# Letting a static scheduler choose ScalarE or VectorE for PSUM read-outs in a gated attention and token-mixing kernel

## The chip, the cores and the metric

The kernel runs on one core of a Trainium2 chip. The metric is the device time of one execution in microseconds; lower is better. Three runs of the kernel before gave 779.43, 781.1 and 781.89 us. A separate execution was recorded by the hardware profiler; all rows of a profile below come from such an execution.

## The reference

Two layers, one after the other, on 8 batches of 3200 tokens and 256 channels. Inputs and output are float32.

```python
scores = (1.0 / S) * np.matmul(z, z.transpose(0, 2, 1))   # z: 8 x 3200 x 64
attn = np.maximum(scores, 0.0) ** 2
x = u * np.matmul(attn, v)                                 # u, v: 8 x 3200 x 256
wq, wk = x @ w_q, x @ w_k                                  # 256 x 64 each
W_tok = (1.0 / np.sqrt(64)) * np.einsum('bsd,btd->bst', wq, wk)
mixed = np.einsum('bst,btd->bsd', W_tok, x)
out = np.maximum(mixed, 0.0) @ w_out                       # 256 x 256
```

The token mixing is linear before its relu, so the kernel never forms the 3200 x 3200 matrix `W_tok`: it sums `wk` transposed times `x` over all tokens into a 64 x 256 matrix per batch (the "heads"), and multiplies the queries by that. The score matrix of the first layer is symmetric, so some of its squared blocks are made once and used a second time, turned by a transposing DMA.

## The kernel before

**Tiling.** The tokens of a batch are cut into 25 tiles of 128 and into seven row groups: six of 512 tokens and one of 128. For each group and tile the scores are one 128 x 512 block. Both products of the first layer contract over 64 of the 128 rows of the array, so matmuls are issued in pairs, one on the upper and one on the lower half of the rows, which run side by side. `scores` (L260) makes a pair of blocks into a PSUM slot of two banks; there are two such slots (`pps`, two buffers), shared with the projections, heads, mixing and output products. `first_stage` (L280) reads the slot into `g` (relu and a scale), on VectorE or ScalarE; `second_stage` (L297) squares `g` to `at` in float16, on ScalarE or GpSimd; `second_product` (L346) multiplies `at` (or a turned block `tt`) by `v` into four accumulator banks: two halves of a row group, each with one bank for each half of the array's rows.

**When a half is complete**, `gate` (L362) copies the first bank to SBUF (`both`, L368), adds the second (L369) on VectorE, and multiplies by `u` on GpSimd (`x_sb`, L388). Only then may the next group write those banks. The group's `x` is turned by a DMA on SyncE's queue (`turn_x`, L396); `projections` (L413) makes queries and keys, `projections_out` (L425) casts them to float16 in `qk` (L430); the keys are turned by another DMA and doubled by GpSimd; `heads` (L449) adds their product with `x` to the sum of the batch. When a batch's sum is known, `mix` (L478) and `mix_out` (L490, the relu, L503) and `proj` and `proj_out` (L505, L521) follow while the next batch's attention runs.

**What sets the order.** The order of every engine's instructions is made at build time by a planner written in the kernel (L575 to L1060). It keeps a clock for TensorE, VectorE, ScalarE and GpSimd (`clock`), adds a fixed weight for each piece of work (`give`), and always places the next accumulation step (`acc_step`), pair of scores (`use_pair`) or extra work (`use_keys`, `use_mix`, `use_projs`) on TensorE as its clocks allow. `shut()` is the time at which the open half will be complete; `calm_for` and `choose` keep engines free around it. On the chip the engines follow that order and wait on semaphores; the planner's clocks play no part there. SyncE's queue carries the loads of `u`, all transposing DMAs and the stores; GpSimd's queue those of `v` and `z`.

**Constants of the planner** that the change touches: `KEEP` (L56) is the number of tiles of a row group held back for its last chunk; `XWAIT` (L856) the time between the expected landing of turned `x` and its projections; `MIXES` (L589) the spacing of the three blocks of mixing behind a batch's heads.

Of the kernel before, what the change touches and what calls it, by code (L numbers as in the profile page):

```python
# [16 lines left out]
def kernel(  # L17
# [35 lines left out]
    NX = 7  # L53
    NXT = 4
    NEARBY = 8
    KEEP = 4  # L56

    consts = ctx.enter_context(tc.tile_pool(name="consts", bufs=1))
    pz = ctx.enter_context(tc.tile_pool(name="pz", bufs=1))
# [237 lines left out]
    def second_stage(p, g, ways):  # L297
        at = pat.tile([P, 2 * W], FP16, tag="at", name="at")
        at0 = 0
        parts = pieces(p)  # L300
        if len(ways) > len(parts):
            parts = [(slice(h, h + 1), parts[0][1]) for h in range(2)]
        for (hs, w), on_act in zip(parts, ways * 2):
            n = hs.stop - hs.start
            out = at[:, at0 : at0 + n * w].rearrange("p (n w) -> p n w", w=w)
            if on_act:
                nc.scalar.square(out=out, in_=g[:, hs, 0:w])  # L307
            else:
                nc.gpsimd.tensor_mul(out=out, in0=g[:, hs, 0:w], in1=g[:, hs, 0:w])  # L309
            at0 += n * w  # L310
        at0, blocks = 0, []
        for tile_ in tiles[2 * p : 2 * p + 2]:
            b, gi, ti = tile_
            made[tile_] = (at, at0)
            gj = group_of(ti)
            if is_turned(b, gi, gj):
                blocks.append((b, gi, gj, ti - starts[gj] // P, 1, at0, at0 + widths[gi]))
            at0 += widths[gi]
        if len(blocks) == 2 and blocks[0][:3] == blocks[1][:3] and blocks[1][3] == blocks[0][3] + 1:
            blocks = [blocks[0][:4] + (2, blocks[0][5], blocks[1][6])]  # L320

        def turn(b, gi, gj, n0, nn, c0, c1):
            if (b, gi, gj) not in turned:
                if gj == LASTG:
                    tag, nr, bufs = "ttl", 1, 8
                else:
                    homes[b, gi, gj] = home = homes_free.pop(0)
                    tag, nr, bufs = f"tt{home}", 4, 1
                turned[b, gi, gj] = ptt.tile([P, nr, 4, P], FP16, tag=tag, name=tag, bufs=bufs)
            out = turned[b, gi, gj][:].rearrange("p n j t -> p (n j) t")  # L330
            nc.sync.dma_start_transpose(out=out[:, 4 * n0 : 4 * (n0 + nn), :], in_=at[:, c0:c1])

        return [(x, lambda x=x: turn(*x)) for x in blocks]
# [25 lines left out]

        return [lambda j=j: [one(j, r) for r in range(2)] for j in js]  # L360

    def gate(b, gi, half):  # L362
        if (b, gi) not in xs:
            assert len(xs) < NX, (b, gi, list(xs))
            xs[b, gi] = px.tile([P, 2, NC, 2, dh], FP16, tag="x_sb", name="x_sb")
        n = min(2, widths[gi] // P - 2 * half)
        both = psum.tile([P, 2 * D], FP32, tag="both", name="both")
        nc.scalar.copy(out=both[:, 0 : n * D], in_=accs[half, 0][:, 0 : n * D])  # L368
        nc.vector.tensor_add(  # L369
            out=both[:, 0 : n * D], in0=accs[half, 1][:, 0 : n * D], in1=both[:, 0 : n * D]  # L370
        )
        if b == last and gi >= LASTG - 2:
            if gi == LASTG - 2 and half == 0:
                spare = pv.tile([P, NT, D], FP16, tag="v_sb", name="xd")
                for i in range(3):
                    xds[LASTG - 2 + i] = spare[:, 4 * i : min(4 * i + 4, 9), :]
            nc.vector.tensor_mul(
                out=xds[gi][:, 2 * half : 2 * half + n, :].rearrange("p n d -> p (n d)"),
                in0=both[:, 0 : n * D],
                in1=us[b, gi][:, 2 * half : 2 * half + n, :].rearrange("p n d -> p (n d)"),  # L380
            )
        u_rows = us[b, gi][:, 2 * half : 2 * half + n, :].rearrange("p n (c d) -> p (n c) d", d=dh)
        if 2 * half + n == widths[gi] // P:
            us.pop((b, gi))

        def make_x():
            for r in [half] if widths[gi] == W else range(2):
                nc.gpsimd.tensor_mul(  # L388
                    out=xs[b, gi][:, 0:n, :, r, :].rearrange("p n c d -> p (n c) d"),
                    in0=both[:, 0 : n * D].rearrange("p (m d) -> p m d", d=dh),  # L390
                    in1=u_rows,
                )

        make_x()
# [27 lines left out]
                    stop=(stop and c == NC - 1),  # L422
                )

    def projections_out(b, gi, ps):  # L425
        xTs.pop((b, gi))
        n = min(2, widths[gi] // P)
        qks[b, gi] = pq.tile([P, 2, HW], FP16, tag="qk", name="qk")
        nr = len(halves(gi))
        nc.scalar.copy(out=qks[b, gi][:, 0:nr, 0 : n * P], in_=ps[:, 0:nr, 0 : n * P])  # L430

    def turn_keys(b, gi):
        nn = widths[gi] // P
# [53 lines left out]
                    stop=(db == ND - 1),  # L487
                )

    def mix_out(b, gi, ps):  # L490
        n = min(2, widths[gi] // P)
        nr = len(halves(gi))
        if b < last:
            rts[b, gi] = prt.tile([P, 2, ND, HW], FP16, tag="rt", name="rt")
        else:
            rt = pat.tile([P, 2 * W], FP16, tag="at", name="rt")
            rts[b, gi] = rt[:].rearrange("p (r d s) -> p r d s", r=2, d=ND)
        out = rts[b, gi][:, :, :, :].rearrange("p r d s -> p r (d s)")[:, 0:nr, 0 : ND * n * P]
        if isinstance(ps, list):
            for r in range(nr):  # L500
                nc.scalar.activation(out=out[:, r, :], in_=ps[r][:, 0 : ND * n * P], func=RELU)
        else:
            nc.scalar.activation(out=out, in_=ps[:, 0:nr, 0 : ND * n * P], func=RELU)  # L503

    def proj(b, gi, banks):  # L505
        rt = rts.pop((b, gi))
# [79 lines left out]
    keys_at, out_of, turned_at, z_at, v_at = {}, {}, {}, {}, {}  # L586
    produced, stored = [0], []
    mixed_at = []
    MIXES = 18.0  # L589
    MIXES_END = 14.0  # L590
    PAIRED = [0, 1, 2, 3, 4, 5]
    last = B - 1
# [80 lines left out]
    def squares():  # L673
        while pending and pending[0][0] <= clock[PE] + 0.3:
            ready, p, g = pending.pop(0)
            a, c = max(clock[ACT], ready), max(clock[POOL], ready)
            on_act = a + SPARE < c and (a + 1.06 <= shut() + LATE or a + 2.5 < c)
            ways = [on_act]
            if clock[PE] < UNTIL and max(a + 0.57, c + 0.97) + SPLIT < min(a + 1.06, c + 1.9):
                ways = [a < c, a >= c]  # L680
                done = max(give(ACT, ready, 0.57), give(POOL, ready, 0.97))
            else:
                done = give(ACT, ready, 1.06) if on_act else give(POOL, ready, 1.9)
            for (b, gi, gj, _, nn, _, _), turn in second_stage(p, g, ways):
                n = nn * widths[gi] // P
                due = done + {1: 4.0, 2: 9.0}.get(gj - gi, FARDUE)
# [23 lines left out]
    def use_keys(b, gi):  # L710
# [8 lines left out]
            heads(*prior, ps, halves(gi))  # L719
            clock[PE] += 0.44 if prior[1] < LASTG else 0.11  # L720
        ready = clock[PE] + FROM_PE
        projections_out(b, gi, ps)
        done = give(ACT, ready, 0.56)
        n = widths[gi] / P
        final = (b, gi) == (last, LASTG - 2)
        if not final:
# [37 lines left out]
    def use_mix(b, gi):  # L764
# [1 line left out]
        ps = ps_tile("mx")  # L766
        mix(b, gi, [ps[:, 0, :], ps[:, 1, :]])
        clock[PE] += 0.22
        mix_out(b, gi, ps)
        done = give(ACT, clock[PE] + FROM_PE, 1.03 if gi < LASTG else 0.3)  # L770
        close_slot(done)
        mixed_at.append((done, b, gi))
        if gi in PAIRED:
# [77 lines left out]
            move(max(t + 2, clock[POOL] + SLACK), t + 7, 0.55, 1.6, lambda: load_u(b + 1, 0))  # L851

    SPARE = 0.3
    BIAS = 0.2
    XDUE = 5.0
    XWAIT = 7.0  # L856
    LATE = 0.3

    def half_done(b, gi, half):
        ready = clock[PE] + FROM_PE  # L860
        t = give(ACT, ready, 0.57)
        t = give(DVE, t, 0.68)
        free_at[half] = t
        if b == last and gi >= LASTG - 2:
            give(DVE, t, 0.75)
        t = give(POOL, t, 1.2)
        gate(b, gi, half)
        if half == halves(gi)[-1]:
            n = 8 if widths[gi] == W else 2
            move(  # L870
# [275 lines left out]
```

## Time and profile before

| what | value |
|---|---|
| runs, median (lowest to highest) | 781.1 us (779.43 to 781.89) |
| span of the profiled execution | 780.0 us |
| its instructions | 28,286 |
| mean granted clock of TensorE | 0.998 |

The page gives the busy time and share of each engine, the chain of work that ended last (followed back from the last instruction to whatever released each step), and groups of instructions by source line with their mean duration and the idle time in front of them. PE is TensorE's matmul, PEld its weight load, DVE VectorE, ACT ScalarE, POOL GpSimd and SP SyncE. Further views used below: busy time of each engine in given stretches of the span (with the granted clock, DMA share and GB/s at the end of the row), waits by line and releaser, the chain in order of time, and the timeline.

### The profile page before, as it was taken

What the parts mean: (1) busy time and instruction counts of PE and PEld (TensorE: products, weight loads), DVE (VectorE), ACT (ScalarE), POOL (GpSimd) and SP (SyncE); (2) the same over time, 40 slices, a digit from 0 to 9 for tenths busy, and PEclk for the clock granted to TensorE, in tenths of its full rate; (3) what the DMA queues carried; (4) which work ended last, traced back from release to release, by engine and by line L of the source; (5) the groups of instructions that cost most, each with busy time, mean ns of one, the idle gap of its engine ahead of it and who ended that gap; (6) DMA issues with size and microseconds to landing.
All of it is one profiled execution on the core that took longest, in us unless ns stands there. A gap on an engine that the chain in (4) does not pass through costs nothing.

```text
span 780.0 us, 28286 instructions
## 1 busy us (share of the span) xinstructions
PE 765.9 (98%) x12410; PEld 674.0 (86%) x12410; DVE 490.5 (63%) x506; ACT 558.1 (72%) x672; POOL 619.5 (79%) x518
## 2 busy tenths in 40 slices
PE   8999999999999999999999999999999999999996
PEld 6889989988888888988889888898888988999894
DVE  6576768767565766655657556575566765656534
ACT  6786785676877776876678777787778578777644
POOL 7798887668986978887779769887888868887850
PEclk9999999999999999999999999999999999999999
DMA  7899999999999999999899999999989999989725
GB/s 181 157 152 175 162 160 170 171 187 180 222 183 190 200 218 204 151 170 217 198 171 193 168 221 168 199 161 171 241 159 208 162 196 211 157 169 168 183 81 198
DMA packets 307116, 141.11 MB, mean 181 GB/s; under 512 B 285744, under 2 KB 288432, under 8 KB 306992
## 3 DMA queue, kind: packets, MB, share of 16 engines
q1 hardware_dynamic: 300224, 123.13, 85.8%
q0 software_dynamic: 6624, 15.98, 14.6%
q8 instruction: 97, 1.59, 0.9%
q14 instruction: 27, 0.22, 0.1%
q10 hardware_dynamic: 144, 0.20, 0.1%
HBM read 59.64 MB, written 26.21 MB: 110 GB/s over the span
## 4 chain that ended last, share of the span: by engine, by line
PE 94%; DVE 2%; DMA 1%; ACT 1%; issue 1%; POOL 0%; DVEq 0%; SPq 0%
PE acc L352 68%; PE sc L265 13%; PE fo L513 6%; PE qk L417 3%; PE qk L454 2%; PE mx L482 1%; DVE g L291 1%; DMA v_sb<-in_v_dram 1%; ACT g L287 1%; DVE both L369 0%; DVE fo L535 0%; DMA z<-in_z_dram 0%; ACT at L307 0%; PE xtx L555 0%; PE hd L454 0%
## 5 line engine op out<-in xcount | busy, mean ns | idle before, releaser
L352 PE MATMUL acc<-v_sb,at 64*128 64x256 f16 x7344 | 506.0, 269 | 2.3 <-issue 1.5
L309 POOL TENSOR_TENSOR at<-g 128x1024 f16<-128x1024 f32 (+2 forms) x240 | 432.5, 1813 | 88.0 <-DVE g L291 46.8
L352 PEld LDWEIGHTS <-at 64*128 64x128 f16 x7344 | 403.9, 94 | 54.5 <-issue 9.7
L291 DVE TENSOR_SCALAR g<-sc 128x1024 f32<-128x1024 f32 (+2 forms) x302 | 349.9, 1175 | 121.8 <-PE sc L265 109.8
L307 ACT ACTIVATE at<-g 128x1024 f16<-128x1024 f32 (+2 forms) x242 | 241.6, 1015 | 25.0 <-DVE g L291 22.5
L287 ACT ACTIVATE g<-sc 128x1024 f32<-128x1024 f32 (+2 forms) x177 | 174.8, 990 | 56.2 <-PE sc L265 50.9
L265 PE MATMUL sc<-zT 64*128 64x512 f16 x924 | 185.3, 375 | 2.4 <-DVE g L291 1.2
L388 POOL TENSOR_TENSOR x_sb<-both,u_sb 128x512 f16<-128x512 f32 (+1 forms) x112 | 134.3, 1205 | 48.9 <-DVE both L369 48.4
L352 PE MATMUL acc<-v_sb,tt 64*128 64x256 f16 x2272 | 168.0, 269 | 0.0
L352 PEld LDWEIGHTS <-tt 64*128 64x128 f16 x2272 | 127.0, 94 | 10.3 <-issue 0.6
L369 DVE TENSOR_TENSOR both<-acc,both 128x512 f32<-128x512 f32 (+1 forms) x104 | 69.5, 670 | 70.9 <-ACT both L368 62.0
L368 ACT COPY both<-acc 128x512 f32<-128x512 f32 (+1 forms) x104 | 58.9, 566 | 66.5 <-PE acc L352 63.1
L265 PEld LDWEIGHTS <-zT 64*128 64x128 f16 x924 | 62.2, 94 | 9.8 <-issue 5.2
L535 DVE TENSOR_SCALAR fo<-fo 128x1024 f32<-128x1024 f32 (+2 forms) x31 | 32.7, 1067 | 41.4 <-PE fo L513 41.3
L503 ACT ACTIVATE rt<-mx 128x1024 f16<-128x1024 f32 (+1 forms) x49 | 45.5, 931 | 12.2 <-PE mx L482 12.0
L430 ACT CAST qk<-qk 128x512 f16<-128x512 f32 (+1 forms) x54 | 29.4, 544 | 29.2 <-PE qk L454 25.4
L513 PE MATMUL fo<-wo,rt 128*128 128x256 f16 x400 | 49.4, 273 | 0.1
L469 DVE TENSOR_TENSOR ha<-qk,ha 128x512 f32<-128x512 f32 x37 | 25.6, 691 | 36.1 <-ACT qk L430 35.8
L513 PEld LDWEIGHTS <-rt 128*128 128x128 f16 x400 | 36.4, 98 | 10.8 <-issue 6.5
L540 ACT ACTIVATE fo<-fo 128x1024 f32<-128x1024 f32 (+2 forms) x27 | 24.6, 914 | 19.8 <-PE fo L513 19.8
L417 PE MATMUL qk<-xT_sb,wqk 64*128 64x256 f16 (+1 forms) x404 | 32.2, 265 | 0.0
L454 PE MATMUL qk<-x_sb,kx 64*128 64x256 f16 x360 | 29.1, 269 | 0.0
(44 smaller groups left out, 237.0 us busy)
## 6 DMA issues: line engine op xcount, KB each, us to landing
u_sb<-in_u_dram SPq DMA_DIRECT2D x48, 512.0 KB, 5.0
out_dram<-fo SPq DMA_DIRECT2D x46, 512.0 KB, 4.4
v_sb<-in_v_dram POOLq DMA_DIRECT2D x35, 320.0 KB, 6.2
zn<-in_z_dram POOLq DMA_DIRECT2D x7, 400.0 KB, 6.3
tt<-at SPq DMA_TRANSPOSE x143, 4.5
u_sb<-in_u_dram SPq DMA_DIRECT2D x8, 128.0 KB, 3.6
out_dram<-fo SPq DMA_DIRECT2D x8, 128.0 KB, 3.5
out_dram<-fo SPq DMA_DIRECT2D x4, 256.0 KB, 4.2
```

Source lines behind the costliest of these rows:

```text
L265: nc.tensor.matmul(out=sc[:, h, 0:gw], lhsT=z_cols(b, h, ti * P, P), rhs=z_cols(b, h, gs, gw), start=True, stop=True,)
L287: nc.scalar.activation(out=g[:, hs, 0:w], in_=sc[:, hs, 0:w], func=RELU, scale=GSCALE)
L291: nc.vector.tensor_scalar(out=g[:, hs, 0:w], in0=sc[:, hs, 0:w], scalar1=0.0, scalar2=GSCALE, op0=AOP.max, op1=AOP.mult,)
L307: nc.scalar.square(out=out, in_=g[:, hs, 0:w])
L309: nc.gpsimd.tensor_mul(out=out, in0=g[:, hs, 0:w], in1=g[:, hs, 0:w])
L352: nc.tensor.matmul(out=accs[half, r][:, ds((j % 2) * D, D)], lhsT=weights(b, gi, ti, j)[top(r), :], rhs=vs[b][top(r), ti, :], start=(first ...
L368: nc.scalar.copy(out=both[:, 0 : n * D], in_=accs[half, 0][:, 0 : n * D])
L369: nc.vector.tensor_add(out=both[:, 0 : n * D], in0=accs[half, 1][:, 0 : n * D], in1=both[:, 0 : n * D])
L388: nc.gpsimd.tensor_mul(out=xs[b, gi][:, 0:n, :, r, :].rearrange("p n c d -> p (n c) d"), in0=both[:, 0 : n * D].rearrange("p (m d) -> p m ...
L417: nc.tensor.matmul(out=ps[:, r, 0 : n * P], lhsT=wqk[top(r), c, :, :].rearrange("p t h -> p (t h)"), rhs=xTs[b, gi][top(r), 0:n, c, :], st ...
L503: nc.scalar.activation(out=out, in_=ps[:, 0:nr, 0 : ND * n * P], func=RELU)
L513: nc.tensor.matmul(out=banks[r][:, ds(j * D, D)], lhsT=flat[:, ds((dc * n + j) * P, P)], rhs=wo[:, dc, :], start=(dc == 0 and j == 0), sto ...
```

## The change

Four pieces of work may now go to either of two engines, by the planner's clocks: the copy of the first accumulator bank, the cast of queries and keys and mixing's relu (ScalarE or VectorE), and the square (ScalarE, GpSimd or, under a margin `MORE`, VectorE). The weights in the planner follow (0.58 and 0.69 for a read-out of 512 columns, 1.28 for the product with `u`, others), and `KEEP`, `XWAIT` and `MIXES` have new values.

```diff
-    KEEP = 4
+    KEEP = 6
...
-            if on_act:
+            if on_act == 1:
                 nc.scalar.square(out=out, in_=g[:, hs, 0:w])
             else:
-                nc.gpsimd.tensor_mul(out=out, in0=g[:, hs, 0:w], in1=g[:, hs, 0:w])
+                mul = nc.vector.tensor_mul if on_act else nc.gpsimd.tensor_mul
+                mul(out=out, in0=g[:, hs, 0:w], in1=g[:, hs, 0:w])
...
-    def gate(b, gi, half):
+    def gate(b, gi, half, by_act):
...
-        nc.scalar.copy(out=both[:, 0 : n * D], in_=accs[half, 0][:, 0 : n * D])
+        copy = nc.scalar.copy if by_act else nc.vector.tensor_copy
+        copy(out=both[:, 0 : n * D], in_=accs[half, 0][:, 0 : n * D])
...
-    def projections_out(b, gi, ps):
+    def projections_out(b, gi, ps, by_act=True):
...
-        nc.scalar.copy(out=qks[b, gi][:, 0:nr, 0 : n * P], in_=ps[:, 0:nr, 0 : n * P])
+        copy = nc.scalar.copy if by_act else nc.vector.tensor_copy
+        copy(out=qks[b, gi][:, 0:nr, 0 : n * P], in_=ps[:, 0:nr, 0 : n * P])
...
-            nc.scalar.activation(out=out, in_=ps[:, 0:nr, 0 : ND * n * P], func=RELU)
+            part = ps[:, 0:nr, 0 : ND * n * P]
+            if by_act:
+                nc.scalar.activation(out=out, in_=part, func=RELU)
+            else:
+                nc.vector.tensor_scalar(out=out, in0=part, scalar1=0.0, scalar2=None, op0=AOP.max)
...
-    MIXES = 18.0
+    MIXES = 14.0
...
-            on_act = a + SPARE < c and (a + 1.06 <= shut() + LATE or a + 2.5 < c)
-            ways = [on_act]
+            d = max(clock[DVE], ready)
+            by_act = a + SPARE < c and (a + 1.06 <= shut() + LATE or a + 2.5 < c)
+            by_dve = d + 1.5 + MORE < (a + 1.06 if by_act else c + 1.9) and d + 1.5 <= shut() + LATE + 0.6
+            ways = [2 if by_dve else by_act]
...
-        projections_out(b, gi, ps)
-        done = give(ACT, ready, 0.56)
+        a, d = (max(clock[x], ready) for x in (ACT, DVE))
+        by_act = a + 0.58 <= d + 0.69 or d + 0.69 > shut() + LATE + 0.6
+        projections_out(b, gi, ps, by_act)
+        done = give(ACT, ready, 0.58) if by_act else give(DVE, ready, 0.69)
...
-        mix_out(b, gi, ps)
-        done = give(ACT, clock[PE] + FROM_PE, 1.03 if gi < LASTG else 0.3)
+        ready = clock[PE] + FROM_PE
+        a, d = (max(clock[x], ready) for x in (ACT, DVE))
+        by_act = a + 1.03 <= d + 1.22 or d + 1.22 > shut() + LATE + 0.6
+        mix_out(b, gi, ps, by_act)
+        if by_act:
+            done = give(ACT, ready, 1.03 if gi < LASTG else 0.38)
+        else:
+            done = give(DVE, ready, 1.22 if gi < LASTG else 0.42)
...
+    MORE = 3.0
...
-    XWAIT = 7.0
+    XWAIT = 2.0
...
-        t = give(ACT, ready, 0.57)
-        t = give(DVE, t, 0.68)
+        a, d = (max(clock[x], ready) for x in (ACT, DVE))
+        by_act = max(a + 0.58 + HOP, d) <= d + 0.69
+        t = give(ACT, ready, 0.58) if by_act else give(DVE, ready, 0.69)
+        t = give(DVE, t, 0.69)
         free_at[half] = t
...
-        t = give(POOL, t, 1.2)
-        gate(b, gi, half)
+        t = give(POOL, t, 1.28)
+        gate(b, gi, half, by_act)
```

More of the change, by code (lines that the diff above doesn't have):

```diff
@@ L682, in squares @@
             else:
[L683 removed]
+                done = give(DVE, ready, 1.5) if by_dve else give(ACT, ready, 1.06) if by_act else give(POOL, ready, 1.9)
             for (b, gi, gj, _, nn, _, _), turn in second_stage(p, g, ways):
```

2 lines of the change are left out of this document (1 added, 1 removed).

## The prediction

> **What bounds the kernel now.** I read the page first (busy shares and the chain that ended last), then the busy time in stretches of 20 us, TensorE's own waits, and the chain and the timeline around each hole.
>
> ```profile
> span 780.0 us, 28286 instructions
> PE 765.9 (98%) x12410; PEld 674.0 (86%) x12410; DVE 490.5 (63%) x506; ACT 558.1 (72%) x672; POOL 619.5 (79%) x518
> PE 94%; DVE 2%; DMA 1%; ACT 1%; issue 1%; POOL 0%; DVEq 0%; SPq 0%
> ```
>
> TensorE is busy for 98% of the span and makes 94% of the chain; no other engine is above 79%. A busy TensorE may still be slow, so its pace is needed: the chain has long unbroken pieces.
>
> ```profile
> 74.15 6.22 PE acc L352 x114
> 115.13 1.49 issue
> ```
>
> 114 matmuls of the second product, two at a time on the two halves of the rows, take 6.22 us: 0.109 us a pair. I call this a pair-time below. All other work is fixed in number (both programs have 12,407 matmuls of the same kinds), so only holes in this stream can go or come. Where they are, the stretches tell (engine columns: busy us of 20, instructions):
>
> ```profile
> 0.00:20.00 20.00, 16.17 (x200) 12.53 (x202) 13.49 (x18) 12.76 (x21) 15.49 (x23) 1.00 0.77 183
> 20.00:40.00 20.00, 19.24 (x316) 16.86 (x314) 11.72 (x13) 13.89 (x20) 13.66 (x11) 1.00 0.90 160
> 40.00:60.00 20.00, 19.69 (x319) 17.95 (x318) 15.37 (x15) 17.64 (x20) 19.28 (x15) 1.00 1.03 147
> 60.00:80.00 20.00, 20.00 (x350) 19.62 (x347) 12.53 (x13) 12.33 (x15) 15.54 (x13) 1.00 1.21 167
> ...
> 100.00:120.00 20.00, 18.51 (x313) 17.22 (x311) 13.13 (x14) 15.34 (x17) 16.20 (x15) 1.00 1.30 167
> ...
> 140.00:160.00 20.00, 19.88 (x330) 18.57 (x327) 13.29 (x15) 13.69 (x17) 12.35 (x12) 1.00 1.18 186
> ...
> 400.00:420.00 20.00, 19.47 (x300) 16.81 (x297) 12.53 (x12) 15.56 (x18) 15.88 (x16) 1.00 1.08 190
> ...
> 500.00:520.00 20.00, 19.93 (x337) 18.91 (x334) 14.07 (x14) 15.64 (x20) 17.16 (x14) 1.00 1.13 200
> ...
> 760.00:780.00 20.00, 13.05 (x122) 8.70 (x118) 9.74 (x14) 8.55 (x18) 1.65 (x2) 0.94 0.52 198
> ```
>
> TensorE idles 3.83 us in the first stretch and 6.95 in the last; the middle has 0.76 + 0.31 + 1.49 + 0.12 + 0.53 + 0.07 = 3.28 us, and every stretch left out shows 20.00. The granted clock (1.00) leaves nothing to explain. The idle time understates a hole: a matmul is drawn 0.269 us long (row below), the next is due 0.109 after its start, so each hole costs 0.16 us beyond what is seen. With about sixteen holes in the middle that is 3.28 + 16 x 0.16 = 5.8 us: the most that any reordering can win there.
>
> ```profile
> L352 PE MATMUL acc<-v_sb,at 64*128 64x256 f16 x7344 | 506.0, 269 | 2.3 <-issue 1.5 <-DMA v_sb<-in_v_dram 0.2 <-DVE both L369 0.2
> PE sc L265 <- DVE g L291: 1.2, 5, 0.4
> PE sc L265 <- ACT g L287: 0.9, 3, 0.4
> ```
>
> Eight waits of the scores show as idle. Two kinds of hole matter. One is the score buffer: there are two PSUM slots, and a pair of scores waits until the first stage has read the slot two places back:
>
> ```profile
> 408.07 0.61 PE L265 MATMUL sc<-zT 64*128 64x512 f16 x4
> 408.50 1.23 DVE L291 TENSOR_SCALAR g<-sc 128x1024 f32<-128x1024 f32 x1 [0.48 <-PE sc L265]
> 409.78 0.69 PE L265 MATMUL sc<-zT 64*128 64x512 f16 x4 [0.23 <-DVE g L291]
> ```
>
> The first pair of scores here (512 columns, so two pair-times) is issued by 408.29 and its slot is free at 409.78: about 1.47 us by VectorE, and some 0.2 less by ScalarE (1,025 against 1,220 ns below). The other is the accumulator: the first half must be copied and the second added to it before the next row group may write there.
>
> **The change, part by part.** The prices of what moves (mean ns behind the busy us):
>
> ```profile
> L368 ACT COPY both<-acc 128x512 f32<-128x512 f32 x96 | 55.9, 582 | 64.0 <-PE acc L352 60.8 <-PE sc L265 2.8
> L369 DVE TENSOR_TENSOR both<-acc,both 128x512 f32<-128x512 f32 x96 | 66.2, 690 | 68.5 <-ACT both L368 59.6 <-PE sc L265 6.5 <-PE fo L513 1.8
> L467 DVE COPY ha<-qk 128x512 f32<-128x512 f32 x8 | 5.5, 689 | 5.7 <-ACT qk L430 5.5
> L430 ACT CAST qk<-qk 128x512 f16<-128x512 f32 x47 | 27.5, 585 | 25.4 <-PE qk L454 21.7 <-PE qk L417 3.3
> L503 ACT ACTIVATE rt<-mx 128x1024 f16<-128x1024 f32 x42 | 42.8, 1022 | 11.6 <-PE mx L482 11.4
> L291 DVE TENSOR_SCALAR g<-sc 128x1024 f32<-128x1024 f32 x281 | 339.1, 1220 | 118.0 <-PE sc L265 108.5 <-POOL at L309 2.3 <-POOL x_sb L388 2.2
> L287 ACT ACTIVATE g<-sc 128x1024 f32<-128x1024 f32 x164 | 168.1, 1025 | 49.3 <-PE sc L265 48.4 <-POOL at L309 0.7
> L307 ACT ACTIVATE at<-g 128x1024 f16<-128x1024 f32 x222 | 231.3, 1056 | 24.5 <-DVE g L291 21.9
> L309 POOL TENSOR_TENSOR at<-g 128x1024 f16<-128x1024 f32 x220 | 414.5, 1894 | 86.1 <-DVE g L291 45.3 <-ACT g L287 32.0 <-issue 4.0
> ```
>
> *Who does what.* Counted in the built order of both programs: 41 of 104 accumulator copies, 9 of 54 casts of queries and keys and 3 of 62 relu pieces go to VectorE; first stages go from 302 + 177 (VectorE + ScalarE) to 294 + 184; eight squares go from GpSimd to ScalarE. No square goes to VectorE: the margin MORE = 3.0 is never met, so that part of the edit is empty and costs nothing. ScalarE loses 41 x 0.582 + 9 x 0.585 + 3 x 1.022 = 32.2 us and gains 7 x 1.025 + 8 x 1.056 + one scaling of about 1.0 = 16.6: some 542 us busy. VectorE gains 53 pieces, 41 x 0.689 + 9 x 0.689 + 3 x 1.22 = 38.1, and loses 8 x 1.22 + 1.2 = 11: about 518. GpSimd loses 8 x 1.894 = 15, to 604. All stay below 78% of the span, hidden under TensorE; none of this is on the path except where a reader is late for a slot. The copy and cast on VectorE are priced by the nearest row, the 689 ns copy of the same shape from PSUM; bounds 582 (ScalarE's copy) and 690 (the two-input add). The planner's changed prices (0.58, 0.69) only follow these rows and cost nothing.
>
> *The accumulator.* Copy on ScalarE and add on VectorE take 0.58 + 0.69, both on VectorE 0.69 + 0.69; with hand-overs, and the 0.16 us by which the last matmul outlives its pair-time, about 1.57 and 1.68 us. So VectorE's way is 0.1 longer, and is taken only where ScalarE would be later. KEEP = 6 instead of 4 holds two more tiles back for the closing chunk, 2 x 2 pair-times = 0.44 us more between the end of half 0 and its next use. Counted in the built order behind the first 20 us, half 0 is rewritten within 16 pair-times (1.75 us) seven times before and once after: five times before at only 12 (1.31 us, short by 0.26), and once after, with VectorE's way (short by 0.37).
>
> *The skill on this.* "ScalarE is closer to PSUM, VectorE is closer to SBUF - use accordingly", says the Trainium skill (Advanced Engine Details and Errata, The Read-Write Bubble), which speaks against 53 PSUM reads on VectorE. The rows agree on the sign, 689 against 582 and 1,220 against 1,022: by the rule the sum would be 53 x about 0.11 = 5.9 us worse, if these reads set the end; by the count of covers they don't.
>
> *The score slots.* From 60 us of TensorE work on, five score pairs follow too closely on their slot's readers before (short by 0.05, 0.05, 0.38, 0.18 and 0.16 us), none after. Three of them make most of the 400 to 420 hole. Below 60 us the balance turns: after, four pairs of scores stand close together near 42 us of TensorE work (about 51 us of the span); one slot is rewritten 6 pair-times (0.66 us) behind a VectorE reader that needs 1.47, a wait of 0.81; the next, 4 pair-times behind ScalarE, is paid by the same wait.
>
> *XWAIT 7 to 2, MIXES 18 to 14.* The projections are placed 5 us earlier behind the landing of transposed x: from the close of the accumulator to their first matmul, the middle distance falls from 222 to 166 pair-times (24.2 to 18.1 us). Cover now:
>
> ```profile
> DMA to landing us min/median/max: 2.3/5.5/12.3
> 106.25 2.18 SPq L400 DMA_TRANSPOSE xT_sb<-x_sb  x1
> 125.13 0.27 PE L417 MATMUL qk<-xT_sb,wqk 64*128 64x128 f16 x2
> ```
>
> The slowest transpose is this one: it lands at 106.25 + 12.3 = 118.6 and is used 6.5 us later. Five us less leave 1.5, so both edits cost 0. Without that cover TensorE itself stands, since it works in order (rival C). The moves on SyncE's queue are the same in number and kind. MIXES pulls the second and third mixing blocks 4 and 8 us forward; a buffer of queries and keys still has over 25 us of TensorE work between its last use and its next writer.
>
> *The sum against the profiled execution.* The 400 to 420 stretch: 0.53 idle + four holes x 0.16 = 1.2, all gone (bounds 0.8 and 1.3). Accumulator shortages elsewhere in the middle: two of 0.26 = 0.5 gone; slot shortages of 0.05 and 0.16 = 0.2 gone. Before 60 us: two shortages of 0.26 and one slot wait of 0.16 gone, 0.37 and 0.81 come: +0.5 (bounds -0.7, if the new crowding is absorbed, and +1.5, if squares behind it come late too). The 1.49 us at 115: no semaphore ended it, the kernel's edits don't touch its cause, and the page says only that TensorE waited for nothing that it shows. It is one event in 780 us; I count it as half gone, (1.49 + 0.16)/2 = -0.8, bounds -1.65 and +1.65 (twice). Together -1.2 - 0.5 - 0.2 + 0.5 - 0.8 = -2.2. The first and last stretches stay: the order is unchanged for the first 230 matmuls (200 of them fill the first 20 us), and the end is built by the same lines. Thus 780.0 - 2.2 = 777.8 of span; the median lies 781.1 - 780.0 = 1.1 above the span: 778.9. The runs spread from 779.43 to 781.89, about the size of one such event, so part of that 1.1 may be the event in the other runs; I lean to 778.6.
>
> The Trainium skill (Runtime: NRT & Kernel Launch, Instruction fetch mechanics) calls fetching instructions "hidden" by the issue floor; by it the 1.49 is no late fetch and the -0.8 would fall out, giving 779.4. The trace can't name the cause, so its half stands.
>
> **The rivals.** *A, forecast: the middle's holes close, the early one moves.* 778.6, own range 776.8 to 780.2.
>
> *B, nothing measurable.* The event without a semaphore comes again (+0.8 on the forecast), and the early crowding costs its upper bound (+1.0): 778.6 + 1.8 = 780.4. For it: in 40 to 60 us GpSimd is busy for 19.28 and ScalarE for 17.64 of 20, more than in any stretch shown. Against: the crowding is one slot.
>
> *C, slower: keys too early.* Place: L417, at the head of TensorE's queue, behind the x transpose on SyncE. It decides once a transpose lands 1.5 us later than the worst now. The DMA share is 1.21 and 1.30 at 60 and 100 us, where a transpose took 12.3 us against a median of 5.5. If five transposes of the first two batches came 3 us later, each would stop everything for 1.5 to 2: five x 1.6 = 8 less the 2.2 won, 781.1 + 5.8 = 786.9; with three, 783.7. For it: the cover goes from 6.5 to 1.5 there. Against: the work on the queue is the same, and most transposes take half as long.
>
> *D, slower: VectorE becomes the accumulator's bound.* Each of 41 copies keeps half 0 about 0.11 us longer, and queues behind a 1.22 us first stage where the clocks are off; one miss in four of 0.6 gives 10 x 0.6 = 6 less 2.2: 784.9. For it: half 0 is the tight one. Against: all but one have 16 pair-times or more for the 1.68 us needed, a spare of 0.07 at the least. The skill's rule on PSUM quoted above would end near here.
>
> **How the numbers follow.** A measurement of this kernel tells about 0.3% (2.3 us) from no change: 778.8 and 783.4 are the edges. A 0.52, B 0.29, C 0.12, D 0.07. Faster: most of A, 0.45 (its centre is just past the edge, its own range on both sides) and 0.02 of B: 0.47. Slower: 0.10 of C, 0.06 of D, 0.01 of B: 0.17. Same: the rest, 0.36. The range goes from 776.0 (the event gone in every run, early crowding absorbed: 778.6 - 0.8 - 1.2, and some tenths) to 783.2 (B and the mild ends of C and D).
>
> **What would show it.** Right: the stretches from 60 to 760 us at 20.00 but for one without a semaphore; a wait of PE sc on DVE g near 51 us; TensorE's waits on ScalarE's first stage and on L369's successor down to one or two; ScalarE near 542 and VectorE near 518 us busy; no square by VectorE. Wrong: an idle TensorE in front of L418 with the x transpose as releaser (C), waits of the accumulator for VectorE's add beyond one (D), new holes behind 60 us waiting for squares, or a granted clock below 1.00.

## The result and the profile after

Four runs of the changed kernel gave a median of 776.94 us (776.21 to 778.79), against 780.97 us for the kernel before (four runs, 779.43 to 781.89). The ratio is 0.9947 with a 95% interval of 0.9926 to 0.9968: 0.53%, about 4 us, faster, and beyond the 0.3% that a measurement of this kernel can tell. Twelve runs on a later occasion gave 0.9968 (0.9953 to 0.9984), 0.32%, which is only at that edge. The forecast was 778.6 us. Where a kernel is timed below, executions that took over 1.5% more than its fastest are left out of its ratio.

The head of the page of the changed kernel, and its chain of waits by engine:

```profile
span 774.4 us, 28287 instructions
PE 762.9 (99%) x12410; PEld 673.8 (87%) x12410; DVE 518.8 (67%) x550; ACT 548.5 (71%) x635; POOL 603.2 (78%) x510
PE 94%; DVE 2%; DMA 2%; POOL 1%; issue 0%; ACT 0%; POOLq 0%; DVEq 0%; SPq 0%
```

The span is 5.6 us shorter than in the profile of before. In each of the four runs of the changed kernel the device time lies 1.8 us above the span (776.21, the fastest, is the run of 774.4); in the later runs of the kernel before it is 1.7 to 1.9. So its 780.0 belongs to a run of about 781.8, near its slowest (781.89), and the median, 780.97, to a span of 779.2. The profiles, one near the slowest run and one of the fastest, therefore differ by more than the medians do (4.0), by about the size of one event that not every execution has (the last section).

Busy time in stretches of the changed kernel (stretches in which nothing is lost are joined):

```profile
0.00:20.00 20.00, 15.74 (x206) 12.53 (x208) 13.41 (x18) 13.04 (x22) 15.73 (x24) 1.00 0.75 183
20.00:40.00 20.00, 19.54 (x327) 17.46 (x323) 13.18 (x16) 13.76 (x17) 14.24 (x11) 1.00 0.98 148
40.00:60.00 20.00, 19.10 (x308) 16.99 (x305) 16.73 (x16) 16.84 (x20) 16.73 (x17) 1.00 1.00 180
60.00:80.00 20.00, 20.00 (x346) 19.59 (x343) 13.12 (x14) 11.81 (x13) 16.39 (x13) 1.00 1.21 188
...
100.00:120.00 20.00, 20.00 (x342) 19.39 (x339) 15.86 (x17) 15.00 (x18) 17.07 (x16) 1.00 1.10 184
...
160.00:380.00 220.00, 220.00 (x3622) 193.06 (x3618) 146.35 (x157) 158.82 (x180) 173.33 (x146) 1.00 1.05 192
400.00:420.00 20.00, 20.00 (x340) 19.08 (x336) 14.40 (x15) 16.38 (x18) 16.61 (x15) 1.00 1.13 220
420.00:500.00 80.00, 79.89 (x1306) 69.70 (x1304) 53.53 (x56) 55.22 (x64) 64.34 (x56) 1.00 0.96 179
...
520.00:760.00 240.00, 240.00 (x3905) 208.89 (x3899) 152.70 (x165) 165.03 (x191) 183.91 (x150) 1.00 0.92 174
```

Behind 60 us TensorE shows 0.11 us of idle time up to 760, where before it showed 1.49 + 0.12 + 0.53 + 0.07 = 2.21. The holes at 115 and in 400 to 420 are gone. The loss in front of 60 us has moved, not shrunk: 0.46 + 0.90 us from 20 to 60, against 0.76 + 0.31. TensorE's waits that concern the steps of the prediction, and two places in its timeline (start, length, instruction, and in brackets the idle time in front and its releaser):

```profile
PE sc L265 <- DVE g L291: 1.4, 3, 0.7
PE sc L265 <- ACT g L287: 0.6, 2, 0.3
...
PE acc L353 <- DVE both L371: 0.2, 1, 0.2
```

```profile
39.18 0.59 PE L353 MATMUL acc<-v_sb,at 64*128 64x256 f16 x7 [0.17 <-DVE both L371]
...
51.12 0.84 PE L265 MATMUL sc<-zT 64*128 64x512 f16 x4 [0.74 <-DVE g L291]
```

The eight waits of scores on a first stage are five. One of them is the crowding near 51 us (0.74 idle; 0.81 was forecast). The one accumulator shortage that the forecast left is there too, at 39 us (0.17 idle + 0.16 = 0.33; 0.37 forecast). A second wait for the add, too short for the list of waits, stands at 55.4 us in both kernels (0.12 us idle before, 0.10 after). The groups of instructions for the pieces that may now choose their engine:

```profile
L370 ACT COPY both<-acc 128x512 f32<-128x512 f32 x59 | 34.5, 584 | 40.6 <-PE acc L353 38.4 <-POOL at L310 0.9 <-POOL x_sb L390 0.7
L370 DVE COPY both<-acc 128x512 f32<-128x512 f32 x37 | 25.6, 691 | 28.3 <-PE acc L353 25.5 <-PE sc L265 2.5
...
L433 DVE CAST qk<-qk 128x512 f16<-128x512 f32 x8 | 5.5, 689 | 2.8 <-PE qk L457 2.7
```

A copy or cast of 512 columns on VectorE takes 689 to 691 ns, at the upper of the two bounds given (582 and 690). No square stands on VectorE.

To set the two traces beside each other I took the start of every matmul, and for the same piece of TensorE work the time lost against a pace of 0.109 us a pair. Lost before and after: 1.62 and 0.02 us around 115, 1.82 and 0.27 around 410, 2.48 and 2.61 from 12 to 48 us of work, 6.31 and 6.03 ahead of that, and 7.39 and 6.43 in all of the rest up to the last 20 us of work, where both lose 2.45. That is 4.3 us together. Another 1.2 lies behind the last computation, which ended 5.85 us ahead of the span's end before and 4.64 after: its stores land sooner. The last nine stores, their issues (first and last start) and their time to landing, before:

```profile
L541 SPq DMA_DIRECT2D out_dram<-fo x9: 332/337/938, 767.5 to 775.4; - x9
...
DMA to landing us min/median/max: 2.9/4.0/4.3
```

And after:

```profile
L548 SPq DMA_DIRECT2D out_dram<-fo x9: 332/333/649, 763.1 to 770.7; - x9
...
DMA to landing us min/median/max: 2.3/2.7/3.1
```

A median of 4.0 us became 2.7. The bytes and the number of stores are the same.

### The profile page after: what moved, and what is told of

It is laid out like the page before. It is cut to its first block, busy times and chain, and to the rows that moved or that the text cites. A ratio compares the mean times of both kernels' runs of the same rounds, so it can differ in the third digit from the quotient of the medians.

```text
span 774.4 us, 28287 instructions
## 1 busy us (share of the span) xinstructions
PE 762.9 (99%) x12410; PEld 673.8 (87%) x12410; DVE 518.8 (67%) x550; ACT 548.5 (71%) x635; POOL 603.2 (78%) x510
## 4 chain that ended last, share of the span: by engine, by line
PE 94%; DVE 2%; DMA 2%; POOL 1%; issue 0%; ACT 0%; POOLq 0%; DVEq 0%; SPq 0%
PE acc L353 69%; PE sc L265 13%; PE fo L520 6%; PE qk L419 3%; PE qk L457 2%; PE mx L485 1%; DMA v_sb<-in_v_dram 1%; DVE g L291 1%; POOL x_sb L390 1%; DMA z<-in_z_dram 0%; DVE fo L542 0%; DMA xT_sb<-x_sb 0%; DVE both L371 0%; POOL at L310 0%; DVE both L370 0%
## 5 line engine op out<-in xcount | busy, mean ns | idle before, releaser
L353 PE MATMUL acc<-v_sb,at 64*128 64x256 f16 x7344 | 500.8, 269 | 1.3 <-POOL at L310 0.8
L310 POOL TENSOR_TENSOR at<-g 128x1024 f16<-128x1024 f32 (+2 forms) x232 | 414.4, 1799 | 84.8 <-DVE g L291 46.3
L291 DVE TENSOR_SCALAR g<-sc 128x1024 f32<-128x1024 f32 (+1 forms) x294 | 341.2, 1181 | 107.5 <-PE sc L265 97.4
L307 ACT ACTIVATE at<-g 128x1024 f16<-128x1024 f32 (+1 forms) x250 | 251.3, 1021 | 27.3 <-DVE g L291 24.1
L287 ACT ACTIVATE g<-sc 128x1024 f32<-128x1024 f32 (+2 forms) x184 | 180.5, 984 | 76.6 <-PE sc L265 72.0
L353 PE MATMUL acc<-v_sb,tt 64*128 64x256 f16 x2272 | 162.7, 269 | 0.0
L370 ACT COPY both<-acc 128x512 f32<-128x512 f32 (+1 forms) x63 | 36.0, 571 | 45.7 <-PE acc L353 41.8
L508 ACT ACTIVATE rt<-mx 128x1024 f16<-128x1024 f32 (+1 forms) x46 | 42.5, 926 | 12.8 <-PE mx L485 12.7
L370 DVE COPY both<-acc 128x512 f32<-128x512 f32 (+1 forms) x41 | 27.3, 665 | 31.3 <-PE acc L353 28.5
L433 ACT CAST qk<-qk 128x512 f16<-128x512 f32 (+1 forms) x45 | 24.4, 542 | 25.3 <-PE qk L457 22.7
```

What stands on the lines that cost most here:

```text
L287: nc.scalar.activation(out=g[:, hs, 0:w], in_=sc[:, hs, 0:w], func=RELU, scale=GSCALE)
L291: nc.vector.tensor_scalar(out=g[:, hs, 0:w], in0=sc[:, hs, 0:w], scalar1=0.0, scalar2=GSCALE, op0=AOP.max, op1=AOP.mult,)
L353: nc.tensor.matmul(out=accs[half, r][:, ds((j % 2) * D, D)], lhsT=weights(b, gi, ti, j)[top(r), :], rhs=vs[b][top(r), ti, :], start=(first ...
L508: nc.scalar.activation(out=out, in_=part, func=RELU)
```

## The experiments

I ask of each kernel what its built order says. The *count*, theory 1 (T1), goes through the order and takes, for every accumulator half and every score slot, the TensorE work between the last use and the next writer; where that is less than the readers need (1.57 or 1.68 us for a half, some 1.27 or 1.47 for a slot) the missing time is a too-early rewrite. Only the sum behind 60 us of TensorE work is used. Ahead of that the count rises from 0.7 us before to 2.1 in the changed kernel, but the time lost there does not (6.31 + 2.48 = 8.8 and 6.03 + 2.61 = 8.6 up to 48 us of work), so there the count fails. By theory 1 the gain is no edit's own: it comes from a placement in which such rewrites don't occur. The count knows nothing of waits on DMAs or on other pieces of work. Theory 2 says that the free choice of engine carries the gain, theory 3 that `KEEP` does, theory 4 that `XWAIT` and `MIXES` do. C and D are the prediction's rivals. Results, with the count behind 60 us and the span of the profiled execution:

| kernel | count, us | span, us | ratio to before (95%) |
|---|---|---|---|
| before | 1.7 | 780.0 | 1 |
| changed | 0 | 774.4 | 0.9947 (0.9926 to 0.9968) |
| changed, measured again | 0 | 774.6 | 0.9968 (0.9953 to 0.9984) |
| engines only | 1.1 | 778.7 | 1.0017 (0.9997 to 1.0036) |
| `KEEP` only | 5.6 | 782.2 | 1.0048 (1.003 to 1.0065) |
| times only | 4.5 | 783.2 | 1.0054 (1.0036 to 1.0072) |
| changed with the old times | 1.1 | 777.4 | 0.9984 (0.9968 to 0.9999) |
| changed with the old `MIXES` | 0 | 777.5 | 0.9975 (0.9957 to 0.9993) |
| keys 3 us earlier still | 1.25 | 777.7 | 1.0033 (1.0005 to 1.0061) |
| all copies on ScalarE | 0.04 | 779.9 | 1.0023 (1.0005 to 1.004) |
| all copies on VectorE | 1.7 | 783.5 | 1.0072 (1.0055 to 1.0088) |
| squares on VectorE | 2.5 | 792.5 | 1.0212 (1.0188 to 1.0237) |
| weights cast early | 0 | – | 0.9982 (0.9964 to 1.0) |
| weights cast early, all copies on ScalarE | 0.04 | 776.8 | 0.9973 (0.9963 to 0.9983) |

**Each part alone.** First the choice of engine and its prices, with the three old constants:

```diff
-    KEEP = 6
+    KEEP = 4
...
-    MIXES = 14.0
+    MIXES = 18.0
...
-    XWAIT = 2.0
+    XWAIT = 7.0
```

> The kernel before with the choice of engine and its prices alone; KEEP 4, XWAIT 7, MIXES 18 as before. Theory 1 (the time follows the places where a score pair or an accumulator half is rewritten too soon behind its reader, counted in the built order): behind 60 us of TensorE work these come to 1.1 us against 1.7 in the kernel before and 0 in the changed one; before 60 us 1.0 against 0.7. So about 780.5 us, half a microsecond from the kernel before. Theory 2 (the choice of engine alone carries the gain): 777 us. VectorE takes some 50 of 104 accumulator copies in either case.

Measured 1.0017 (0.9997 to 1.0036): no gain, and theory 2 falls. Theory 1 misses too, if barely: by the count this kernel should be half a microsecond faster than before (0.9993), just outside the interval. Its profiled execution (780.45 us), second fastest of twelve, holds one event without a semaphore, of 1.34 us (the last section); what the slower ones lost isn't known. Then the kernel before with one group of constants each:

```diff
-    KEEP = 4
+    KEEP = 6
```

> The kernel before with KEEP = 6 alone. Theory 1: the count of too early rewrites behind 60 us of work rises to 5.6 us (score slots 4.8, accumulators 0.7) against 1.7, and before 60 us to 1.2 against 0.7: slower, about 785 us. Theory 3 (holding back two more tiles is what helps, since it covers the accumulator's read-out): 778 to 779 us.

```diff
-    MIXES = 18.0
+    MIXES = 14.0
...
-    XWAIT = 7.0
+    XWAIT = 2.0
```

> The kernel before with XWAIT = 2 and MIXES = 14 alone. Theory 1: the count rises to 4.5 us behind 60 us of work (accumulators 3.1, score slots 1.4) against 1.7, and 1.6 against 0.7 before: slower, about 784.5 us. Theory 4 (earlier projections and mixing carry the gain): 777 to 778 us. If keys come before their transposed x (rival C of the prediction), TensorE waits at the projections with the x transpose as releaser; I expect none.

Both are slower than before, 1.0048 and 1.0054, near what the count gave; theories 3 and 4 fall. TensorE's waits in the kernel with `KEEP` alone:

```profile
PE sc L265 <- DVE g L291: 3.4, 7, 0.8
...
PE acc L352 <- DVE both L369: 1.0, 3, 0.5
```

Seven waits on VectorE's first stage instead of five, and three on the accumulator's add: two more tiles held back don't shorten the waits for the accumulator by themselves, though the prediction's 0.44 us would suggest that they do. The same edit inside the changed kernel does no harm, since the other choices have moved everything else. The fourth takes only the times back out of the changed kernel:

```diff
-    MIXES = 14.0
+    MIXES = 18.0
...
-    XWAIT = 2.0
+    XWAIT = 7.0
```

> The changed kernel with XWAIT = 7 and MIXES = 18 again. Theory 1: 1.1 us of too early rewrites behind 60 us of work against 0, 2.4 against 2.1 before: about 778.3 us. Theory 4: back to 781. If neither edit matters: 776.9 us.

Measured 0.9984 (0.9968 to 0.9999), between before and changed, as the count said (1.1 us). The interval touches that of the changed kernel's second measurement, so that the times carry part of the gain is likely and not proved. With only `MIXES` set back:

```diff
-    MIXES = 14.0
+    MIXES = 18.0
```

> The changed kernel with MIXES = 18 again, XWAIT = 2 kept. Count: 0 behind 60 us of work as in the changed kernel, 2.1 before. Theory 1: as the changed kernel within 1 us. If the spacing of mixing carries the 2.3 us that undoing both times cost: 779 us.

Its ratio, 0.9975 (0.9957 to 0.9993), can't be told from the changed kernel's. But its trace shows two projections that wait for the x transpose, 0.41 us at 131 and 0.50 at 206, which the count of 0 doesn't hold:

```profile
PE qk L419 <- DMA xT_sb<-x_sb: 0.9, 2, 0.5
```

**The count and the traces.** Against the pace of 0.109 us a pair, TensorE loses between 50 and 735 us of its work 6.7 and 6.6 us in the two traces of the changed kernel (count 0), 8.5 in changed with the old times (1.1), 10.3 with the engines only (1.1, and 1.5 by the event), 10.8 before (1.7, and 1.6 by the event), 12.6 with `KEEP` only (5.6), 13.8 with the times only (4.5), but 9.5 with the old `MIXES` (0). So more too-early rewrites go with more time lost, and the count alone doesn't give its size.

**Rival C: how much cover do the projections have?** `XWAIT` goes from 2 to −1 for all batches but the first and the last:

```diff
-            add_extra(t + (XWAIT if b < last else 0.0), "keys", lambda: use_keys(b, gi))
+            add_extra(t + (0.0 if b == last else -1.0 if b else XWAIT), "keys", lambda: use_keys(b, gi))
```

> The changed kernel with XWAIT = -1 instead of 2 for all batches but the first: projections are placed 3 us earlier behind the expected landing. In the changed kernel's trace the projections of seven groups in the second and third batch come only 0.2 to 3 us behind the landing of their x. Rival C of the prediction (keys too early cost TensorE): waits at the projections with the x transpose as releaser, together about 8 us; 777 + 8 = 785 us. The count of too early rewrites alone (0.7 + 0.55 us behind 60 us of work against 0) gives 778.2 us.

Measured 1.0033 (1.0005 to 1.0061), about 5 us slower than the changed kernel's second measurement; the count gives 1.25 of that. The profiled execution, one of the fastest (779.45 us), shows 0.2 us of waiting for the x transpose, so where the rest went in the others it can't say; that it is rival C's price is not shown.

**Rival D: VectorE as the accumulator's bound.** All 104 copies on one engine, in the changed kernel:

```diff
-        by_act = max(a + 0.58 + HOP, d) <= d + 0.69
+        by_act = True
```

> The changed kernel with all 104 accumulator copies on ScalarE; casts, relu and constants as changed. Count of too early rewrites: 0.04 us behind 60 us of work against 0, 2.3 against 2.1 before. Theory 1: about 777.2 us, no difference that can be told. If the copies on VectorE carry the gain: 780 to 781 us.

```diff
-        by_act = max(a + 0.58 + HOP, d) <= d + 0.69
+        by_act = False
```

> The changed kernel with all 104 accumulator copies on VectorE. Count: 0.6 (accumulators) + 1.1 (score slots) behind 60 us of work against 0, 2.9 against 2.1 before 60 us. Theory 1: 777 + 2.5 = 779.5 us. Rival D of the prediction (VectorE's read-out holds the accumulator): more than ten waits of TensorE for VectorE's add, 783 us or more.

The first is a miss: a count of 0.04 us, yet 1.0023. Its trace names the cause, in TensorE's waits and timeline:

```profile
PE qk L419 <- POOL wqk L207: 1.6, 2, 1.0
PE acc L353 <- DMA v_sb<-in_v_dram: 1.5, 2, 1.2
...
PE qk L419 <- DMA xT_sb<-x_sb: 0.6, 1, 0.6
```

```profile
45.64 0.28 PE L419 MATMUL qk<-xT_sb,wqk 64*128 64x256 f16 x1 [1.03 <-POOL wqk L207]
46.44 0.61 PE L419 MATMUL qk<-xT_sb,wqk 64*128 64x256 f16 x7 [0.53 <-POOL wqk L207]
```

The first projection of all waits for GpSimd to cast the weights of the projections (L207). Neither the planner nor my count has that dependency, nor the landing of `v` and x. The kernel with all copies on VectorE has it too (1.7 us), and beside it rival D's mechanism, small:

```profile
PE sc L265 <- DVE g L291: 2.2, 6, 0.6
PE qk L419 <- POOL wqk L207: 1.7, 2, 1.1
...
PE acc L353 <- DVE both L371: 1.2, 3, 0.5
```

1.0072 (1.0055 to 1.0088) is above the time that D gives (784.9, a ratio of 1.0049) and 6 us above the count's, but the add accounts for three waits and 1.2 us where D wanted ten of 0.6. To separate the weights from the copies, the cast is brought forward, alone and with all copies on ScalarE (then with the edit above as well):

```diff
-        at_time(40.0, cast_weights)
+        at_time(32.0, cast_weights)
```

> The changed kernel with the cast of the projection weights given to GpSimd at 32 us of the planner's clock instead of 40, so some 8 us before the first projection (0.3 us before it in the changed kernel's trace). Count of too early rewrites: 0 behind 60 us of work as in the changed kernel, 1.8 against 2.1 before 60 us. Theory 1: 0 to 0.5 us faster than the changed kernel, and no execution that waits at the first projection.

> All 104 accumulator copies on ScalarE as before in the experiment on that, with the weights' cast at 32 us. There TensorE stood at the first projection for GpSimd's cast (1.6 us idle in two waits). Theory 1: with that wait gone, 781.7 - 2.4 = 779.3 us or less; count 0.04 behind 60 us of work, 2.6 before. If the copies on VectorE are what carries the gain: no better than 781.

With the weights early, all copies on ScalarE cost 0.9973 (0.9963 to 0.9983), which can't be told from the changed kernel's 0.9968 measured beside it; without, 1.0023. So the miss was the weights' cast, and sending 41 copies to VectorE gains nothing that can be measured. Bringing the cast forward alone gains nothing (0.9982). The only profiled execution of that kernel took 790.95 us, is not in its ratio, and is read only for what its two long waits are:

```profile
PE acc L353 <- issue: 4.5, 1, 4.5
PE qk L419 <- DMA xT_sb<-x_sb: 4.1, 1, 4.1
```

The second is rival C's mechanism, once: the transpose is issued at 70.2 us and lands 8.6 later, at 78.8, where the changed kernel's was issued at 64.8 and landed at 70.3, 3.6 ahead of its use at 73.9. Being 8.5 late it uses up that cover, and TensorE stands for 4.1. The wait stands only where `XWAIT` is low: from 60 to 760 us none of the four traces with 7 (before, engines only, `KEEP` only, changed with the old times) has a wait of TensorE for an x transpose, and five of the ten with 2 or −1 have: 0.13 us (times only), 0.19 (keys earlier), 0.65 (copies on ScalarE), 0.41 and 0.50 (old `MIXES`) and these 4.1.

**The part that the change leaves empty.** `MORE` = 0 lets squares go to VectorE (121 of them do, 115 of 128 x 1024):

```diff
-    MORE = 3.0
+    MORE = 0.0
```

> The changed kernel with MORE = 0: VectorE takes 121 squares of 128 x 1024, which it takes none of in the changed kernel. Outputs stay the reference's. Count: 2.5 us behind 60 us of work against 0, 0.9 against 2.1 before: 778.3 us if VectorE's square takes about the 1.24 us of its other pieces of that size (1.5 in the planner) and disturbs nobody. If VectorE and GpSimd block each other at two SBUF inputs (the Trainium skill, SBUF - State Buffer, Who interferes with whom): squares of 2 us and more on VectorE or longer ones on GpSimd, VectorE late for score slots, 790 us or more.

1.0212, by far the slowest. 3.2 us of that are waits for the weights' cast as above, in two waits. The groups of the squares in that kernel:

```profile
L310 POOL TENSOR_TENSOR at<-g 128x1024 f16<-128x1024 f32 x165 | 342.9, 2090 | 96.9 <-ACT g L287 78.8 <-DVE g L291 9.2 <-issue 8.0
L310 DVE TENSOR_TENSOR at<-g 128x1024 f16<-128x1024 f32 x115 | 186.1, 1623 | 16.2 <-ACT g L287 14.2
```

VectorE's timeline ahead of TensorE's longest hole, then GpSimd's, then TensorE's:

```profile
259.15 4.67 DVE L310 TENSOR_TENSOR at<-g 128x1024 f16<-128x1024 f32 x1
263.74 1.21 DVE L291 TENSOR_SCALAR g<-sc 128x1024 f32<-128x1024 f32 x1
264.88 1.21 DVE L310 TENSOR_TENSOR at<-g 128x1024 f16<-128x1024 f32 x1
```

```profile
258.39 1.28 POOL L390 TENSOR_TENSOR x_sb<-both,u_sb 128x512 f16<-128x512 f32 x1
259.63 1.89 POOL L310 TENSOR_TENSOR at<-g 128x1024 f16<-128x1024 f32 x1
261.48 1.26 POOL L390 TENSOR_TENSOR x_sb<-both,u_sb 128x512 f16<-128x512 f32 x1
265.03 2.81 POOL L310 TENSOR_TENSOR at<-g 128x1024 f16<-128x1024 f32 x1 [2.30 <-DVE g L291]
```

```profile
265.01 0.61 PE L419 MATMUL qk<-xT_sb,wqk 64*128 64x256 f16 x8 [2.70 <-DVE g L291]
```

The square of 264.88, begun while GpSimd stands idle, takes 1.21 us. That of 259.15 begins while GpSimd works without a break until 261.48 + 1.26 = 262.74, and ends at 263.82, 1.08 later: so it seems to have done next to nothing until then. The other way round, GpSimd's square of 265.03 takes 2.81 us, its own 1.89 and about what VectorE's square had left. The mean of VectorE's square is 1.623, and GpSimd's rises from 1.894 in the kernel before to 2.090. The first stage queued behind the long square (263.74) is late, and TensorE stands 2.70 us for its slot. The Trainium skill (SBUF — State Buffer, Who interferes with whom) says that an instruction of VectorE with two inputs in SBUF contends with a GpSimd instruction that reads SBUF; this run agrees.

**The changed kernel again,** beside the last three:

> The changed kernel once more, unaltered, beside the other three of this call. Ratio to the kernel before 0.994 to 0.997 (777 to 778 us where the kernel before has 780.3). In its trace: no TensorE wait over 0.8 us behind the first 20 us, unless the instruction queue's packet comes late; then one hole of 1.3 to 1.5 us that no semaphore ended.

0.9968 (0.9953 to 0.9984), and a trace that agrees with the first to 0.1 us in nearly every stretch. None of the others beats it, and those with `XWAIT` = 2 and a count near 0, with the weights early or the old `MIXES`, can't be told from it.

## Why the prediction was right, step by step

**The bound and the form of the gain: right.** TensorE's stream sets the time; no engine but TensorE came above 78%, and VectorE and GpSimd were forecast within 1 us (518 and 604 against 518.8 and 603.2), ScalarE within 7 (542 against 548.5). With 53 more pieces read by VectorE, the 5.9 us that these reads would cost if they set the end did not appear: the kernel with the weights early and all copies on ScalarE is no faster than the changed one. Both pages count 12,410 matmuls, not the 12,407 of the prediction; the number is the same in both, and nothing hangs on it.

**The terms of the sum.** Each with what the matching of the two traces gives:

| term | predicted, us | measured, us |
|---|---|---|
| hole in 400 to 420 | −1.2 | −1.55 |
| accumulator and slot shortages elsewhere in the middle | −0.7 | −1.0 |
| before 60 us | +0.5 | −0.15 (the opening −0.28, the rest +0.13) |
| the 1.49 us at 115 | −0.8 | −1.6 |
| the end | 0 | −1.2 |
| sum, from one profiled execution to the other | −2.2 | −5.6, of which 0.1 is not assigned |
| around the span | +1.1 | +1.8 |

The closing of the middle is right in place and size: behind 60 us only 0.11 us of visible idle time is left. The new crowding at 51 us came as forecast, with 0.74 idle; what the early stretch saves elsewhere nearly makes up for it. Three sizes were off. The event at 115 was counted as half gone since it could come again, and it was away in both profiles of the changed kernel. That it is not the edits' doing is argued from where it comes in other kernels (the last section), not shown: the kernel before was profiled once. The end was taken as built by the same lines, so 0: the lines are the same, but the order that they build is not, and the stores land sooner each time that this order runs (the last section). And the 1.1 around the span set the median of three runs against a profile of one of the slowest, where 1.8 is what a run has beside its span. That error has the other sign, so the forecast ended 1.7 above the measured median. Of the 5.6 us between the profiles the forecast's own mechanism, the slots and the accumulator, carries 2.7; the event was a hedge that came out well, and the end was not foreseen.

**The chances.** 0.45 of A's 0.52 stand under faster, though A's centre, 778.6, lies only 0.2 past the edge of 778.8 and its own range reaches up to 780.2: by that range little more than half of it belongs there. That the median came out well past the edge owes something to the event and the end, and the second measurement is close to the edge.

**Edits priced at nothing.** `MORE`: right, no square on VectorE, and the run with it open shows that the margin keeps some 19 us away (1.0212 against 0.9968), the 3.2 of the weights' cast among them. `XWAIT` and `MIXES`: no stall, right, but the cover was mis-sized. I said that the worst one keeps 1.5 us. The x transpose issued at 123.3 in the changed kernel, and the projection that reads it (the first and last start behind the durations):

```profile
L402 SPq DMA_TRANSPOSE xT_sb<-x_sb x1: 1807/1807/1807, 123.3 to 123.3; - x1
...
DMA to landing us min/median/max: 6.4/6.4/6.4
```

```profile
L419 PEld LDWEIGHTS <-wqk x8: 94/94/95, 129.8 to 130.2; 64*128 64x128 f16 x8
```

It lands at 123.3 + 6.4 = 129.7 and is read at 129.8: 0.1 us, not 1.5. I had subtracted five from the slowest transpose of before, though the order around it changes as well, and the slowest was not the tightest: the one issued at 104.1 there lands at 114.1 and is read at 119.9, a cover of 5.8. In the second execution of the changed kernel the place has 0.3 us. That it stopped TensorE in neither is luck; five kernels next to this one show the wait. And I named one cover only. There is a second one, that of the weights' cast. In GpSimd's timeline of the changed kernel:

```profile
41.66 1.54 POOL L207 CAST wqk<-w32s 64x256 f16<-64x256 f32 x4
```

And in TensorE's:

```profile
43.45 0.68 PE L419 MATMUL qk<-xT_sb,wqk 64*128 64x256 f16 x8
```

The cast ends at 43.2, the first projection starts at 43.45. Three kernels that place the work around it slightly differently lost 1.6, 1.7 and 3.2 us there.

**The rivals.** B, 780.4, is outside the measured ratio's interval. C: the mechanism is real, and its price is paid in kernels next to this one, not in this one. D: the wait is real when all the copies go to VectorE, with three waits; with 41 there is one new in its size, at 39 us, of 0.17, beside the 0.10 at 55 us that before has too.

## What to carry to other kernels

When a change turns several constants of a static scheduler at once, price the order that it builds, not the constants: here each part alone was the same or slower (1.0017, 1.0048, 1.0054) and all together faster (0.9947 and 0.9968). The time by which slots are rewritten too early, counted in the built order, told the two slowest of these parts rightly (785 and 784.5 us expected, 784.26 and 785.45 measured) and missed where something else held TensorE. That count must hold every producer, the casts of weights and the landing of DMAs too, as a placement that is tight on all that it models becomes limited by what it doesn't. Read the median against what a run has beside its span, not against the one execution that was profiled.

## What the runs showed of the hardware

**TensorE stood where its instructions came late.** The instruction queue of the page (q8) brings 97 packets of 16 KB in 780 us, one in about 8 us. In the kernel before, the queues from 100.9 to 114.2 us, just ahead of the hole of 1.49 us at 115.13, were these:

```profile
q1 hardware_dynamic: 2901, 1.40, 64.3%
q0 software_dynamic: 212, 0.54, 38.2%
```

There is no line of q8 in 13.3 us. In the changed kernel in the same stretch:

```profile
q1 hardware_dynamic: 3543, 1.84, 62.1%
q0 software_dynamic: 223, 0.58, 33.7%
q8 instruction: 1, 0.02, 0.5%
```

The kernel with the engines only has such a gap again, elsewhere: no packet of q8 from 154 to 166.8 us, and then

```profile
169.59 0.28 PE L353 MATMUL acc<-v_sb,at 64*128 64x256 f16 x2 [1.34 <-issue]
```

These holes are the only ones above 1 us in the middle that no semaphore ended, but for the 4.5 us of the execution of 790.95 us shown above. The Trainium skill (Runtime: NRT & Kernel Launch, Instruction fetch mechanics) calls the fetch hidden; if the gap is the cause, it was not hidden here, for 1.3 to 1.5 us in two executions of different kernels, at different places. Three smaller ones (0.18, 0.19 and 0.12 us) stand in the traces with all copies on ScalarE, the same with the weights early, and the old `MIXES`. In all six TensorE goes on 2.3 to 2.7 us after the start of a q8 packet that came 11.5 to 16.0 us behind the one before it. A long gap is not enough, though: before, 13.3 us without a packet, up to 315.0, passed with less than 0.1 us lost. That a late packet makes the hole fits all six and wasn't tried by itself. Why it comes late stays open; the other queues took about as much of their engines' time in the changed kernel's stretch (62.1% and 33.7%), where one came.

**The last stores' landing differs by half** (4.0 and 2.7 us at the median) at the same size and number, and that was 1.2 us of the span. It is not chance: from the end of the last computation to the end of the span it is 4.63 to 4.64 us in four traces (changed twice, weights early, old `MIXES`), and 5.09 to 5.85 in the other ten. In these four SyncE issues the nine stores within 8.1 us, in the others that issue nine in a row within 8.4 to 8.7. So it comes with the built order; what in it does this wasn't tried.
